# Banded attention on de-interleaved positions (even, then odd), with the band mask added by a small matmul instead of multiplied in

## The chip, the cores and the metric

One core of one Trainium2 chip. The metric is the device time of one execution in microseconds (us); lower is better. A figure "median (lowest to highest, n runs)" comes from repeated executions. Spans are from the profiled execution, which leaves out some start and end cost, so a span is about 2 us below the time.

Engines: PE is the matmul array, PEld its weight loads, DVE the vector engine, ACT the activation engine, POOL the GpSimd engine, SP the engine that here only issues DMAs. "SPq" is SP's instruction queue.

## The reference

The output is `g*a + (1-g)*b` over 2048 positions of 640 features. `a` is a gated long convolution, done with FFTs. `b` is attention of 32 heads of 20 features, in which a query looks at 8 keys, two positions apart:

```python
W, dil = 8, 2
q, k, v = qkv[0], qkv[1], qkv[2]              # each [1, 32 heads, 2048, 20]
off = jnp.arange(W) * dil
idx = pos[:, None] - off[None, :]             # keys p, p-2, ..., p-14
mask = idx >= 0
...
logits = jnp.where(mask[None, None, :, :], logits, -1e9)
attn = _softmax(logits, axis=-1)
```

The query and its keys always have the same parity. If all even positions are stored first and then all odd ones, the 8 keys are neighbours.

## The kernel before

The kernel has three stages: projections (q, k, v by matmul, and beside them a short convolution on DVE that makes `kv`), attention, and the FFT convolution. The parts that matter follow. The framework orders the instructions of every engine when the kernel is built, and it finds by itself which instruction has to wait for which: two instructions that touch the same tile are tracked by the region that each accesses.

```python
# projections; q32 and k32 are [128, 8, 2080] tiles: 4 heads x 32 rows, 8 head groups t, columns = positions
...
concurrent[1](conc_pools)        # emits the short convolution: kh loads on POOL's queue, multiply-adds on DVE
nc.gpsimd.tensor_copy(VW[:, :, :, DH], valid[:].unsqueeze(2).to_broadcast([128, NB, H]))
for t32 in (q32, k32):           # zero pads, 16 columns on either side
    nc.gpsimd.memset(t32[:, :, 0:HALO], 0.0)
    nc.gpsimd.memset(t32[:, :, HALO + S:XW], 0.0)

for which, dst in ((0, q32), (1, k32)):
    for ft in range(NDT):
        stg = pst.tile([128, S], BF, name="stg", tag="stg")          # two staging buffers
        for sc in range(4):
            ps = pp1.tile([128, 512], F32, name="pj", tag="pj", bufs=2)
            ...                                                      # five matmuls into ps
            nc.scalar.copy(stg[:, 512 * sc:512 * sc + 512], ps[:])
        for h in ...:                                                # scatter: one head's rows to its place
            nc.sync.dma_start(out=dst[32 * h4 + da:32 * h4 + da + n, t, HALO:HALO + S], in_=stg[pa:pa + n, :])
    ...
for b in range(NB):                                                  # V: 18 blocks of 128 keys
    ...                                                              # matmuls into psv, ACT copies to VW

# attention; one step = 4 blocks of 114 queries x 4 heads, 40 steps
def emit_scores(si):
    ...
    for half in range(2):                                            # two heads each
        sc = pp2.tile([128, 2, 512], F32, name=f"sc{half}", tag=f"sc{half}", bufs=1)
        for bb, b in enumerate(blocks):
            for hh in range(2):
                nc.tensor.matmul(sc[:, hh, bb * BP:bb * BP + BP], lhsT=k32[...], rhs=q32[...],
                                 start=True, stop=True, tile_position=(32 * h4, 0), skip_group_check=True)
        nc.scalar.activation(dst, src, ACT.Exp, scale=SCALE)
        nc.vector.tensor_tensor(dst, dst, band[...], ALU.mult)       # zero everything outside the band
...
    fin = pos_.tile([128, D], BF, name="fin", tag="fin")             # in out_proj
    nc.scalar.activation(fin[:], op[:, 0:D], ACT.Copy, scale=omg[:, sb:sb + 1])
```

The softmax here doesn't subtract the row's maximum and nothing guards it: scores larger than these inputs give would overflow.

## Time and profile before

402.21 us median (401.27 to 403.07, 3 runs); span of the profiled run 400.5 us. The stages, read from the timelines of ACT and DVE:

| stage | ends with | us |
|---|---|---|
| projections | last copy of q or k to `stg` starts | 105.7 |
| attention | last `fin` starts | 231.6 |
| FFT | end of the span | 400.5 |

SP's timeline shows the scatters. Columns of the timelines: start in us, length of the stretch, engine, source line, operation, destination and source, how many.

```profile
30.73 43.89 SPq L388 DMA_DIRECT2D q<-stg  x36
75.91 35.59 SPq L388 DMA_DIRECT2D k<-stg  x36
```

The table of stretches gives busy time by engine (in brackets the number of instructions), the granted PE clock, the DMA share and the bandwidth:

```profile
core 0: us, PE busy (x) PEld busy (x) DVE busy (x) ACT busy (x) POOL busy (x), PEclk, DMA share, GB/s
...
60.00:80.00 20.00, 18.04 (x106) 8.95 (x105) 14.11 (x9) 10.03 (x17) 2.21 (x5) 1.00 0.66 143
80.00:106.00 26.00, 17.65 (x62) 6.78 (x61) 25.18 (x12) 7.02 (x13) 10.16 (x13) 0.80 0.59 102
```

In attention, ACT's timeline shows one pair of exps per step; in brackets stands how long the engine had been idle and what released it:

```profile
156.18 1.75 ACT L460 ACTIVATE ET<-sc 128x912 bf16<-128x912 f32 x2 [0.28 <-PE sc L454]
158.41 1.75 ACT L460 ACTIVATE ET<-sc 128x912 bf16<-128x912 f32 x2 [0.48 <-PE sc L454]
160.81 1.75 ACT L460 ACTIVATE ET<-sc 128x912 bf16<-128x912 f32 x2 [0.64 <-PE sc L454]
```

A step takes 2.2 to 2.4 us, of which ACT waits about 0.5 us for scores. The groups of instructions that the change removes or moves (busy us, mean ns of one, idle time before them):

```profile
L461 DVE TENSOR_TENSOR ET<-ET,band 128x912 bf16<-128x912 bf16 (+1 forms) x80 | 45.4, 570 | 14.5 <-ACT ET L460 13.3
...
L426 ACT ACTIVATE fin<-op,omg 128x640 bf16<-128x640 f32 x16 | 12.7, 794 | 27.7 <-PE op L423 19.7
```

### The profile page before, as it was taken

How to read it: one execution, taken by the hardware profiler on the slowest of the kernel's cores; microseconds unless marked ns; L12 is line 12 of the kernel's file. 1: busy time of each engine (PE TensorE's matmuls, PEld its weight loads, DVE VectorE, ACT ScalarE, POOL GpSimd, SP SyncE). 2: the span in 40 equal slices, each digit the busy share in tenths (PEclk: the TensorE clock that was granted, in tenths of full speed). 3: DMA queues.
4: the chain of work that ended last, by engine and by line, in shares of the span. 5: the costliest groups of instructions: out<-in, count | busy, mean ns of one | idle time of the engine just before them, and what ended most of it. 6: DMA issues, size and time to landing. Idle time of an engine off the chain costs nothing. (4 is left out here: it accounts for less than half of the span.)

```text
span 400.5 us, 9049 instructions
## 1 busy us (share of the span) xinstructions
PE 274.8 (69%) x3958; PEld 183.9 (46%) x3958; DVE 229.0 (57%) x294; ACT 194.6 (49%) x302; POOL 91.8 (23%) x97
## 2 busy tenths in 40 slices
PE   0699999875543697978878676861766784787640
PEld 0465555332222465555545345641653573476630
DVE  0331094999698867666685307649753538083540
ACT  1025545422543758585875282860446391936310
POOL 5029502090005300000000061000046008102840
PEclk9999999989655568685859596785696697769695
DMA  8926997575334901010101079999000000000047
GB/s 235 283 75 108 163 183 172 111 156 63 68 112 90 173 19 36 18 52 2 51 2 50 34 259 275 231 291 138 0 3 2 2 2 2 2 2 4 2 95 169
DMA packets 26552, 37.37 MB, mean 93 GB/s; under 512 B 15616, under 2 KB 21364, under 8 KB 26000
## 3 DMA queue, kind: packets, MB, share of 16 engines
q1 hardware_dynamic: 21136, 19.62, 20.8%
q0 software_dynamic: 5232, 17.13, 19.7%
q8 instruction: 31, 0.51, 0.6%
q14 instruction: 9, 0.07, 0.1%
q10 hardware_dynamic: 144, 0.04, 0.0%
HBM read 26.26 MB, written 5.25 MB: 79 GB/s over the span
## 5 line engine op out<-in xcount | busy, mean ns | idle before, releaser
L460 ACT ACTIVATE ET<-sc 128x912 bf16<-128x912 f32 (+1 forms) x80 | 63.9, 855 | 21.2 <-PE O L476 11.0
L376 PE MATMUL pj<-xT,W 128*128 128x512 bf16 x200 | 49.9, 405 | 10.0 <-ACT stg L379 10.0
L308 POOL TENSOR_TENSOR a_lin<-a_lin,b_lin 128x480 bf16<-128x480 bf16 (+1 forms) x18 | 32.8, 1856 | 104.1 <-DVE a_lin L307 104.1
L461 DVE TENSOR_TENSOR ET<-ET,band 128x912 bf16<-128x912 bf16 (+1 forms) x80 | 45.4, 570 | 14.5 <-ACT ET L460 13.3
L190 PE MATMUL pb<-Am,Gre 64*128 64x80 bf16 x512 | 32.4, 233 | 27.4 <-DVE Hs L244 14.7
L196 ACT CAST Am<-pa 128x512 bf16<-128x512 f32 x80 | 41.2, 725 | 17.4 <-PE pa L190 17.4
L454 PE MATMUL sc<-q,k 20*128 20x114 bf16 x576 | 32.0, 257 | 18.8 <-ACT ET L460 17.7
L190 PEld LDWEIGHTS <-Gim 64*128 64x128 bf16 x512 | 27.9, 119 | 31.7 <-issue 31.7
L196 ACT CAST Cm<-pa 128x512 bf16<-128x512 f32 x40 | 21.0, 612 | 42.7 <-PE pa L190 42.7
L244 DVE TENSOR_TENSOR Hs<-pb,Dg 128x960 bf16<-128x960 f32 (+1 forms) x24 | 23.9, 1041 | 29.5 <-PE pb L190 29.4
L379 ACT CAST stg<-pj 128x512 bf16<-128x512 f32 x40 | 22.6, 589 | 30.8 <-PE pj L376 20.1
L376 PEld LDWEIGHTS <-W 128*128 128x128 bf16 x200 | 20.3, 103 | 35.5 <-issue 16.0
L423 PE MATMUL op<-wo,oT 128*128 128x512 bf16 (+1 forms) x160 | 33.1, 362 | 3.4 <-ACT fin L426 3.4
L190 PE MATMUL pb<-Am,Gim 64*128 64x80 bf16 x512 | 33.1, 235 | 0.0
L476 PE MATMUL O<-VW,ET 128*128 128x21 bf16 x576 | 22.4, 179 | 13.1 <-DVE o_S L485 12.8
L406 ACT CAST VW<-psv 128x640 bf16<-128x640 f32 x18 | 12.6, 700 | 36.5 <-PE psv L404 36.5
L307 DVE TENSOR_TENSOR a_lin<-pa,a_lin 128x480 bf16<-128x480 f32 (+1 forms) x24 | 13.3, 591 | 28.9 <-PE pa L190 28.9
L190 PEld LDWEIGHTS <-Gre 64*128 64x128 bf16 x512 | 28.7, 119 | 1.1 <-issue 0.8
L476 PEld LDWEIGHTS <-ET 128*128 128x128 bf16 x576 | 19.3, 102 | 18.3 <-issue 12.7
L454 PEld LDWEIGHTS <-k 20*128 20x128 bf16 x576 | 16.7, 107 | 23.2 <-issue 17.9
L190 PE MATMUL pa<-MU,Up 128*128 128x128 bf16 x160 | 24.0, 252 | 3.3 <-DVE a_lin L307 3.3
L426 ACT ACTIVATE fin<-op,omg 128x640 bf16<-128x640 f32 x16 | 12.7, 794 | 27.7 <-PE op L423 19.7
(76 smaller groups left out, 502.8 us busy)
## 6 DMA issues: line engine op xcount, KB each, us to landing
h_lin<-in_A_v_dram POOLq DMA_DIRECT2D x4, 640.0 KB, 16.2
h_lin<-in_A_ssm_k_dram POOLq DMA_DIRECT2D x8, 320.0 KB, 6.7
b_scr<-fin SPq DMA_DIRECT2D x16, 160.0 KB
W<-in_B_wqkv_dram SPq DMA_DIRECT2D x3, 800.0 KB
kh<-in_A_k_dram POOLq DMA_DIRECT2D x12, 190.0 KB, 13.1
q<-stg SPq DMA_DIRECT2D x28, 80.0 KB
k<-stg SPq DMA_DIRECT2D x28, 80.0 KB
Him<-ca_Him POOLq DMA_DIRECT2D x1, 2048.0 KB, 17.7
```

The lines of the kernel that those rows point to most:

```text
L190: inst = nc.tensor.matmul(*args, **kwargs)
L196: nc.scalar.copy(dst, src)
L244: nc.vector.tensor_tensor(Hs[:, :, :, j0:j0 + nj, :], view, Dgv.unsqueeze(3).to_broadcast([128, 2, IL, nj, 4]), ALU.add)
L307: nc.vector.tensor_tensor(reg, yv, reg, ALU.mult)
L308: (nc.vector if g == NG - 1 else nc.gpsimd).tensor_tensor(reg, reg, breg, ALU.add)
L376: nc.tensor.matmul(ps[:], lhsT=W[:, dt, which, 128 * ft:128 * ft + 128], rhs=xT[:, dt, HALO + 512 * sc:HALO + 512 * sc + 512], start=(dt = ...
L379: nc.scalar.copy(stg[:, 512 * sc:512 * sc + 512], ps[:])
L423: nc.tensor.matmul(op[:, n0:n1], lhsT=oT[:, ft, HALO + 128 * sb:HALO + 128 * sb + 128], rhs=wo[:, ft, n0:n1], start=(ft == 0), stop=(ft == ...
L454: nc.tensor.matmul(sc[:, hh, bb * BP:bb * BP + BP], lhsT=k32[32 * h4:32 * h4 + DH, t, kc:kc + 128], rhs=q32[32 * h4:32 * h4 + DH, t, qc:qc ...
L460: nc.scalar.activation(dst, src, ACT.Exp, scale=SCALE)
L461: nc.vector.tensor_tensor(dst, dst, band[:].unsqueeze(1).unsqueeze(1).to_broadcast([128, 2, nbb, BP]), ALU.mult)
L476: nc.tensor.matmul(O[:, slot * 21:slot * 21 + 21], lhsT=ET[:, h4, bb, :], rhs=VW[:, b, h, :], start=True, stop=True, skip_group_check=True)
```

## The change

The intent is to take DVE's 80 band multiplies away. With even positions stored before odd ones, 8 adjacent keys are needed instead of 8 of 15, so a block of 128 keys serves 121 queries instead of 114, and 17 blocks do instead of 18. The band is added before the exp: a matmul with 11 rows puts 0 inside the band and a large negative number outside it into the score banks, and the score matmuls accumulate on top. `fin` moves from ACT to DVE. The q and k tiles get three pads (front, between the halves, tail) of 7, 7 and 10 columns, and every scatter now writes two runs of 1024 columns. The diff, cut to its core:

```diff
-BP = 114
-NB = 18
-HALO = 16
-XW = 2080
+BP = 121
+NB = 17
+PRE = 7
+HS = 1024 + PRE
+XW = 2072
+NF = 11
+PADS = ((0, PRE), (HS, HS + PRE), (2 * HS, XW))
...
         for t32 in (q32, k32):
-            nc.gpsimd.memset(t32[:, :, 0:HALO], 0.0)
-            nc.gpsimd.memset(t32[:, :, HALO + S:XW], 0.0)
+            for c0, c1 in PADS:
+                nc.gpsimd.memset(t32[:, :, c0:c1], 0.0)
...
-                    nc.sync.dma_start(out=dst[32 * h4 + da:32 * h4 + da + n, t, HALO:HALO + S], in_=stg[pa:pa + n, :])
+                    rows = slice(32 * h4 + da, 32 * h4 + da + n)
+                    o2 = dst[rows, t, PRE:PRE + 2 * HS].rearrange("p (two c) -> p two c", two=2)[:, :, 0:S // 2]
+                    nc.sync.dma_start(out=o2, in_=stg[pa:pa + n, :].rearrange("p (two c) -> p two c", two=2))
...
-            nc.scalar.activation(fin[:], op[:, 0:D], ACT.Copy, scale=omg[:, sb:sb + 1])
+            nc.vector.tensor_scalar(fin[:], op[:, 0:D], omg[:, sb:sb + 1], None, ALU.mult)
...
-            ETb = p2.tile([128, 4, 4, 128], BF, name=f"ET{e_}")
-            nc.gpsimd.memset(ETb[:, :, :, BP:128], 0.0)
+            ETb = p2.tile([128, 2, 512], BF, name=f"ET{e_}")
+            nc.gpsimd.memset(ETb[:], 0.0)
...
-            for half in range(2):
-                sc = pp2.tile([128, 2, 512], F32, name=f"sc{half}", tag=f"sc{half}", bufs=1)
-                for bb, b in enumerate(blocks):
-                    for hh in range(2):
-                        ...                                           # scores of one half
-                nc.scalar.activation(dst, src, ACT.Exp, scale=SCALE)
-                nc.vector.tensor_tensor(dst, dst, band[:]..., ALU.mult)
+            scs = [pp2.tile([128, 2, 512], F32, name=f"sc{half}", tag=f"sc{half}", bufs=1) for half in range(2)]
+            for h4 in range(4):                                       # masks of all four heads
+                nc.tensor.matmul(scs[h4 // 2][:, h4 % 2, 0:nw], lhsT=mk[32 * h4:32 * h4 + NF, :],
+                                 rhs=mq[32 * h4:32 * h4 + NF, 0:nw], start=True, stop=False, ...)
+            for bb, b in enumerate(blocks):
+                for h4 in range(4):                                   # scores of all four heads
+                    nc.tensor.matmul(scs[h4 // 2][:, h4 % 2, bb * BP:bb * BP + BP], ..., start=False, stop=True, ...)
+            for half in range(2):
+                nc.scalar.activation(ETs[(2 * si + half) % NET][:, :, 0:nw], scs[half][:, :, 0:nw],
+                                     ACT.Exp, scale=SCALE)
```

More of the change, by code (lines that the diff above doesn't have):

```diff
@@ L68, in phase_a_consts, with ccol @@
                 Hre=_np_bf16(Hre), Him=_np_bf16(Him))
+def ccol(sb):
+    return PRE + 128 * sb + (PRE if sb >= 8 else 0)
 def phase_b_consts():
-    kl = np.arange(128)[:, None]
-    pl = np.arange(BP)[None, :]
-    dlt = kl - pl
-    band = ((dlt >= 0) & (dlt <= 14) & (dlt % 2 == 0)).astype(np.float32)
-    b = np.arange(NB)[None, :]
-    key = BP * b - 14 + np.arange(128)[:, None]
-    valid = ((key >= 0) & (key < S)).astype(np.float32)
-    ident = np.eye(128, dtype=np.float32)
-    return dict(band=_np_bf16(band), valid=_np_bf16(valid), ident=_np_bf16(ident))
+    B, C = 32768.0, 65536.0
+    kk = np.arange(128); qq = np.arange(BP)
+    kc = kk // 8 - 8; ko = kk % 8; qc = qq // 8 - 8; qo = qq % 8
+    sk = np.where(kc % 2 == 0, 1.0, -1.0); sq = np.where(qc % 2 == 0, 1.0, -1.0)
+    mk = np.zeros((4, 32, 128)); mq = np.zeros((4, 32, BP))
+    mk[:, 0] = kc * kc; mk[:, 1] = kc; mk[:, 2] = 1.0
+    mq[:, 0] = -B; mq[:, 1] = B * (2 * qc + 1); mq[:, 2] = -B * (qc * qc + qc) - C / 2
+    for v in range(8):
+        mk[:, 3 + v] = sk * (ko == v)
+        mq[:, 3 + v] = (C / 2) * sq * np.where(v < qo, -1.0, 1.0)
+    tot = np.einsum("fk,fq->kq", mk[0], mq[0])
+    dlt = kk[:, None] - qq[None, :]
+    inb = (dlt >= 0) & (dlt <= 7)
+    assert (tot[inb] == 0).all() and (tot[~inb] <= -C / 2).all()
+    for m in (mk, mq):
+        assert (_np_bf16(m).astype(np.float64) == m).all()
+    pos = BP * np.arange(NB)[None, :] - PRE + kk[:, None]
+    valid = (((pos >= 0) & (pos < 1024)) | ((pos >= HS) & (pos < HS + 1024))).astype(np.float32)
+    return dict(mk=_np_bf16(mk.reshape(128, 128)), mq=_np_bf16(np.tile(mq.reshape(128, BP), (1, 4))),
+                valid=_np_bf16(valid), ident=_np_bf16(np.eye(128)))
 def lin_src(x2, cq):
@@ L338, in b_proj @@
         W = p1.tile([128, NDT, 3, D], BF, name="W")
-        nc.gpsimd.memset(xT[:, :, 0:HALO], 0.0)
-        nc.gpsimd.memset(xT[:, :, HALO + S:XW], 0.0)
+        for c0, c1 in PADS:
+            nc.gpsimd.memset(xT[:, :, c0:c1], 0.0)
         with nc.allow_non_contiguous_dma(reason="tiny gate_w load"):
@@ L346, in b_proj @@
             xS = pxs.tile([128, 16, D], BF, name="xS")
-            xq4 = xq.rearrange("(t p) d -> p t d", p=128)
+            xq4 = xq.rearrange("(t p two) d -> p two t d", p=128, two=2)
             for c_ in range(4):
                 eng = nc.sync if c_ % 2 == 0 else nc.gpsimd
-                eng.dma_start(xS[:, 4 * c_:4 * c_ + 4, :], xq4[:, 4 * c_:4 * c_ + 4, :])
+                par, t0 = c_ // 2, 4 * (c_ % 2)
+                eng.dma_start(xS[:, 4 * c_:4 * c_ + 4, :], xq4[:, par, t0:t0 + 4, :])
             for w_ in range(3):
@@ L358, in b_proj @@
                         nc.tensor.transpose(trp[:, k_, :], xS[:, sb, 128 * dt:128 * dt + 128], ident[:, :])
-                    nc.vector.tensor_copy(xT[:, dt, HALO + 1024 * grp:HALO + 1024 * grp + 1024],
+                    nc.vector.tensor_copy(xT[:, dt, ccol(8 * grp):ccol(8 * grp) + 1024],
                                           trp[:].rearrange("p a b -> p (a b)"))
@@ L366, in b_proj @@
         for t32 in (q32, k32):
-            nc.gpsimd.memset(t32[:, :, 0:HALO], 0.0)
-            nc.gpsimd.memset(t32[:, :, HALO + S:XW], 0.0)
+            for c0, c1 in PADS:
+                nc.gpsimd.memset(t32[:, :, c0:c1], 0.0)
         for which, dst in ((0, q32), (1, k32)):
@@ L376, in b_proj @@
                         nc.tensor.matmul(ps[:], lhsT=W[:, dt, which, 128 * ft:128 * ft + 128],
-                                         rhs=xT[:, dt, HALO + 512 * sc:HALO + 512 * sc + 512],
+                                         rhs=xT[:, dt, ccol(4 * sc):ccol(4 * sc) + 512],
                                          start=(dt == 0), stop=(dt == NDT - 1))
@@ L392, in b_proj @@
                     for dt in range(NDT):
-                        nc.tensor.matmul(gps[:, sb:sb + 1], lhsT=xT[:, dt, HALO + 128 * sb:HALO + 128 * sb + 128],
+                        nc.tensor.matmul(gps[:, sb:sb + 1], lhsT=xT[:, dt, ccol(sb):ccol(sb) + 128],
                                          rhs=wg[:, dt:dt + 1], start=(dt == 0), stop=(dt == NDT - 1))
@@ L396, in b_proj @@
                 nc.vector.tensor_scalar(omg[:], g_sb[:], -1.0, 1.0, ALU.mult, ALU.add)
-                nc.gpsimd.dma_start(g_scr.rearrange("(t p) -> p t", p=128), g_sb[:])
+                for par in range(2):
+                    nc.gpsimd.dma_start(g_scr.rearrange("(t p two) -> p two t", p=128, two=2)[:, par, :],
+                                        g_sb[:, 8 * par:8 * par + 8])
         for b in range(NB):
-            c0 = HALO + BP * b - 14
+            c0 = BP * b
             psv = pp1.tile([128, 1024], F32, name="psv", tag="psv", bufs=2)
@@ L406, in b_proj, with b_attn @@
             nc.scalar.copy(VW[:, b, :, 0:DH], psv[:, 0:D].rearrange("p (h d) -> p h d", h=H))
-def b_attn(tc, B_wo, q32, k32, VW, omg, band, ident, b_scr):
+def b_attn(tc, B_wo, q32, k32, VW, omg, mk, mq, ident, b_scr):
     nc = tc.nc
+    b_rows = b_scr.rearrange("(t p two) d -> two t p d", p=128, two=2)
     with ExitStack() as es2:
@@ L422, in out_proj @@
                 for ft in range(NDT):
-                    nc.tensor.matmul(op[:, n0:n1], lhsT=oT[:, ft, HALO + 128 * sb:HALO + 128 * sb + 128],
+                    nc.tensor.matmul(op[:, n0:n1], lhsT=oT[:, ft, ccol(sb):ccol(sb) + 128],
                                      rhs=wo[:, ft, n0:n1], start=(ft == 0), stop=(ft == NDT - 1))
             fin = pos_.tile([128, D], BF, name="fin", tag="fin")
-            nc.scalar.activation(fin[:], op[:, 0:D], ACT.Copy, scale=omg[:, sb:sb + 1])
-            nc.sync.dma_start(b_scr[128 * sb:128 * sb + 128, :], fin[:])
@@ L429, in b_attn @@
-        NET = 3
+            nc.vector.tensor_scalar(fin[:], op[:, 0:D], omg[:, sb:sb + 1], None, ALU.mult)
+            nc.sync.dma_start(b_rows[sb // 8, sb % 8], fin[:])
+        NET = 6
         ETs = []
         for e_ in range(NET):
-            ETb = p2.tile([128, 4, 4, 128], BF, name=f"ET{e_}")
-            nc.gpsimd.memset(ETb[:, :, :, BP:128], 0.0)
+            ETb = p2.tile([128, 2, 512], BF, name=f"ET{e_}")
+            nc.gpsimd.memset(ETb[:], 0.0)
             ETs.append(ETb)
-        n_groups = (NB + 3) // 4
@@ L436, in b_attn @@
-        steps = [(bg, t) for bg in range(n_groups) for t in range(NT)]
+        GROUPS = [[0, 1, 2, 3], [4, 5, 6, 7], [8, 9, 10], [11, 12, 13], [14, 15, 16]]
+        steps = [(bg, t) for bg in range(len(GROUPS)) for t in range(NT)]
         o_S_tiles = {}
-        def blocks_of(bg):
-            return list(range(4 * bg, min(4 * bg + 4, NB)))
         def emit_scores(si):
             bg, t = steps[si]
-            blocks = blocks_of(bg)
-            nbb = len(blocks)
-            ET = ETs[si % NET]
-            for half in range(2):
-                sc = pp2.tile([128, 2, 512], F32, name=f"sc{half}", tag=f"sc{half}", bufs=1)
-                for bb, b in enumerate(blocks):
-                    for hh in range(2):
-                        h4 = 2 * half + hh
-                        kc = HALO + BP * b - 14
-                        qc = HALO + BP * b
-                        nc.tensor.matmul(sc[:, hh, bb * BP:bb * BP + BP],
-                                         lhsT=k32[32 * h4:32 * h4 + DH, t, kc:kc + 128],
-                                         rhs=q32[32 * h4:32 * h4 + DH, t, qc:qc + BP],
-                                         start=True, stop=True, tile_position=(32 * h4, 0), skip_group_check=True)
-                src = sc[:, :, 0:nbb * BP].rearrange("p h (b c) -> p h b c", b=nbb)
-                dst = ET[:, 2 * half:2 * half + 2, 0:nbb, 0:BP]
-                nc.scalar.activation(dst, src, ACT.Exp, scale=SCALE)
-                nc.vector.tensor_tensor(dst, dst, band[:].unsqueeze(1).unsqueeze(1).to_broadcast([128, 2, nbb, BP]), ALU.mult)
@@ new lines, in emit_scores @@
+            blocks = GROUPS[bg]
+            nw = len(blocks) * BP
+            scs = [pp2.tile([128, 2, 512], F32, name=f"sc{half}", tag=f"sc{half}", bufs=1) for half in range(2)]
+            for h4 in range(4):
+                nc.tensor.matmul(scs[h4 // 2][:, h4 % 2, 0:nw], lhsT=mk[32 * h4:32 * h4 + NF, :],
+                                 rhs=mq[32 * h4:32 * h4 + NF, 0:nw], start=True, stop=False,
+                                 tile_position=(32 * h4, 0), skip_group_check=True)
+            for bb, b in enumerate(blocks):
+                for h4 in range(4):
+                    nc.tensor.matmul(scs[h4 // 2][:, h4 % 2, bb * BP:bb * BP + BP],
+                                     lhsT=k32[32 * h4:32 * h4 + DH, t, BP * b:BP * b + 128],
+                                     rhs=q32[32 * h4:32 * h4 + DH, t, PRE + BP * b:PRE + BP * b + BP],
+                                     start=False, stop=True, tile_position=(32 * h4, 0), skip_group_check=True)
@@ L463, in emit_pv @@
+            for half in range(2):
+                nc.scalar.activation(ETs[(2 * si + half) % NET][:, :, 0:nw], scs[half][:, :, 0:nw],
+                                     ACT.Exp, scale=SCALE)
         def emit_pv(si):
             bg, t = steps[si]
-            blocks = blocks_of(bg)
+            blocks = GROUPS[bg]
             nbb = len(blocks)
-            ET = ETs[si % NET]
             if t == 0:
@@ L471, in emit_pv @@
             O = pp2.tile([128, 512], F32, name="O", tag="O", bufs=1)
-            for bb, b in enumerate(blocks):
-                for h4 in range(4):
-                    h = 4 * t + h4
+            for h4 in range(4):
+                ET = ETs[(2 * si + h4 // 2) % NET]
+                for bb, b in enumerate(blocks):
                     slot = bb * 4 + h4
-                    nc.tensor.matmul(O[:, slot * 21:slot * 21 + 21], lhsT=ET[:, h4, bb, :], rhs=VW[:, b, h, :],
-                                     start=True, stop=True, skip_group_check=True)
+                    nc.tensor.matmul(O[:, slot * 21:slot * 21 + 21], lhsT=ET[:, h4 % 2, BP * bb:BP * bb + 128],
+                                     rhs=VW[:, b, 4 * t + h4, :], start=True, stop=True, skip_group_check=True)
             nsl = nbb * 4
@@ L489, in emit_group_tail @@
         def emit_group_tail(bg):
-            blocks = blocks_of(bg)
+            blocks = GROUPS[bg]
             o_S = o_S_tiles.pop(bg)
@@ L495, in emit_group_tail @@
                     nc.tensor.transpose(tr[:, ft, 0:BP], o_S[0:BP, bb, 128 * ft:128 * ft + 128], ident[0:BP, 0:BP])
-                nc.vector.tensor_copy(oT[:, :, HALO + BP * b:HALO + BP * b + BP], tr[:, :, 0:BP])
-            pos_done = min(BP * (blocks[-1] + 1), S)
-            while 128 * (sb_done[0] + 1) <= pos_done:
+                nc.vector.tensor_copy(oT[:, :, PRE + BP * b:PRE + BP * b + BP], tr[:, :, 0:BP])
+            done = BP * (blocks[-1] + 1) + PRE
+            while sb_done[0] < 16 and ccol(sb_done[0]) + 128 <= done:
                 out_proj(sb_done[0])
@@ L509, in b_attn @@
                 emit_group_tail(bg)
-        sb_done = sb_done[0]
-        assert sb_done == 16
+        assert sb_done[0] == 16
 @with_exitstack
@@ L536 @@
     CB = phase_b_consts()
-    band_d = nc.inline_tensor(CB["band"], name="band_c")
+    mk_d = nc.inline_tensor(CB["mk"], name="mk_c")
+    mq_d = nc.inline_tensor(CB["mq"], name="mq_c")
     valid_d = nc.inline_tensor(CB["valid"], name="valid_c")
@@ L553 @@
             VW = pb0.tile([128, NB, H, 21], BF, name="VW")
-            band = pb0.tile([128, BP], BF, name="band")
+            mk = pb0.tile([128, 128], BF, name="mk")
+            mq = pb0.tile([128, 4 * BP], BF, name="mq")
             valid = pb0.tile([128, NB], BF, name="valid")
             ident = pb0.tile([128, 128], BF, name="ident")
-            nc.gpsimd.dma_start(band[:], band_d.ap())
+            nc.gpsimd.dma_start(mk[:], mk_d.ap())
+            nc.gpsimd.dma_start(mq[:], mq_d.ap())
             nc.gpsimd.dma_start(valid[:], valid_d.ap())
@@ L563 @@
                                               a_prefetch(tc, A_ssm_k, cd, h_lin, F1bd))))
-            b_attn(tc, B_wo, q32, k32, VW, omg, band, ident, b_scr)
+            b_attn(tc, B_wo, q32, k32, VW, omg, mk, mq, ident, b_scr)
         a_fft(tc, A_q, A_ssm_D, cd, kv, h_lin, F1bd, g_scr, b_scr, out)
```

## The prediction

> What bounds the kernel now. Three stages follow each other: projections (to 106 us), attention (106 to 231.5, where the last output-projection matmul ends), FFT (231.5 to 400.5). The FFT's tables load only when attention frees its memory, so what moves 231.5 moves the end. Inside attention the timeline shows no saturated engine: ACT's exp pair of a 4-block step takes 1.75 us, and one step takes 2.2 to 2.3 us with 0.5 to 0.6 us of ACT waiting for score matmuls (the score banks have one buffer per half). The band multiply (80 x 570 ns, 45 us of DVE, by the groups) is only partly on that loop. At 116 to 125.5 attention stands still: DVE finishes the convolution's kv product (ends 123.9), bands in between.
>
> What changes.
> Removed: 45 us of band on DVE, 12.7 us of `fin` on ACT (goes to DVE, where 640 elements should also take about 0.8 us). Exp area (17x121 against 18x114) and the 40 steps stay.
> Added: 160 mask matmuls, 484 or 363 columns. Two heads of a half run side by side (the trace's 114-column scores come every 25 ns warm, half their streaming time; the Trainium skill, "TensorE: Matmul & The Clock Gate", Part 3, describes such row-group concurrency). At the 0.5 clock that most attention windows show, I estimate 0.40 us per 4-block half, 0.30 per 3-block half.
> Moved, by the static order of instructions: (a) in PE order the last score of half 0 stands behind the masks and most scores of half 1, which wait for the previous exp of half 1. So per 4-block step ACT waits about 0.15+0.40+0.35+0.22 = 1.1 us cold, 0.75 warm; step 2.95 or 2.6 us against 2.25 before. 3-block steps alternate between this and a clean order: about 2.05 cold, 1.8 warm. (b) The six probability buffers are now cleared wholly (about 1.05 us each, from 657 ns for 640 columns), and POOL does it after the eight filter loads (1.19 us each), which wait for kv. The first exp waits for that. With V blocks issued before the rest of q, q scatters leave the loads' way and DVE has no bands in between, so kv should end near 111 (123.9 before); first exp near 122, fourth step near 129, against 126 before. (c) The tail has three blocks and three output projections instead of two: 4 us more, cold.
>
> Sum from the fourth step on: 5 x 2.95 + 28 + 3 x 21 = 106 us mainly cold, 93 us if wholly warm, then a tail of 13 or 11 us: attention ends at 248 or 233, against 231.5. I expect mostly cold, some warm windows around output projections: about 240.
>
> Predicted: 411 us, 80% range 400 to 422. Faster by over 2%: 0.05; within 2%: 0.45; slower by over 2%: 0.50.
>
> What would show it: the groups show no band line; ACT's exps start near 122 after waiting for POOL's clears; ACT waiting for score matmuls grows from 10 us to 25 or more; projections end no later than 106; PE busier in attention; FFT stage as long as before (169 us).
>
> What would make it wrong: the clock gate opening because masks keep the array busy (then 400 to 404); exp not really waiting for the clears, or kv ending much earlier, near 105; masks of two heads not overlapping (then 420 and more); scatters of q and k in 2 KB pieces slower than in 4 KB ones (now about 0.3 us per 4 KB packet), which would delay projections.

## More of the kernel before

The scatters of q begin at 30.73 us, while the projections still run. POOL's timeline says when the pads of q and k are cleared; in brackets stands how long the engine had been idle and what released it.

```profile
79.91 2.75 POOL L121 DMA_DIRECT2D kh<-in_A_k_dram  x4 [15.35 <-DVE tmp L133]
82.64 0.58 POOL L141 DMA_DIRECT2D F1bd<-ca_F1bd  x1
83.26 5.04 POOL L365 COPY VW<-valid 128x576 bf16<-128x576 bf16 x1
87.88 0.53 POOL L367 MEMSET q<- 128x128 bf16 x1
```

The pads of q are cleared at 87.88 us, 57 us after the first scatter into the same tile. They come so late because POOL takes its instructions in order, and the loads of `kh` in front of them wait for DVE (POOL is idle for 15.35 us before them). It costs nothing here: pads and data are different columns, and nothing waits for the clears until attention.

From 60 to 80 us PE is busy for 18.04 of 20 us, at full clock.

## The result

453.86 us median (448.89 to 454.87, 6 runs) against 401.62 us (400.55 to 403.07, 6 runs) for the kernel before; the ratio is 1.126, 95% interval 1.120 to 1.132. The result is numerically correct. Ratios in this document are the mean time of one kernel's fast runs over that of the other's of the same rounds, so not quite the ratio of the medians beside them. The prediction of 411 us, range 400 to 422, was wrong.

| stage | before | after | difference |
|---|---|---|---|
| projections, until the last `stg` copy starts | 105.7 | 149.4 | +43.7 |
| attention, from there until the last `fin` starts | 125.9 | 132.2 | +6.3 |
| rest, to the end of the span | 168.9 | 167.6 | -1.3 |
| span | 400.5 | 449.2 | +48.7 |

Nearly all of the loss is in the projections, where the change adds no work. SP's timeline of the changed kernel, then the line of SP's waits that is new (us in total, times, longest):

```profile
79.75 35.81 SPq L409 DMA_DIRECT2D q<-stg  x36
115.67 39.97 SPq L409 DMA_DIRECT2D k<-stg  x36
```

```profile
SPq L409 <- POOL k L387: 46.4, 1, 46.4
```

The first scatter goes at 79.75 us instead of 30.73. It is one wait of 46.4 us, on POOL's line 387, which is the clear of the q and k pads. The name in that line is the tile that POOL cleared last there; the count that the first scatter really waits for is read further down. POOL's timeline shows why the clear is late:

```profile
71.39 2.74 POOL L139 DMA_DIRECT2D kh<-in_A_k_dram  x4 [12.26 <-DVE tmp L151]
74.13 0.58 POOL L159 DMA_DIRECT2D F1bd<-ca_F1bd  x1
74.75 4.87 POOL L384 COPY VW<-valid 128x544 bf16<-128x544 bf16 x1
79.21 0.60 POOL L387 MEMSET q<- 128x56 bf16 x3
```

POOL's queue is as before; the clear is even 8.7 us earlier (79.21 against 87.88). What is new is that somebody waits for it. One waiting scatter holds all 36: SP issues in order. This is what the Trainium skill says in "DMA: Bandwidth & Descriptors", section "Anatomy of one DMA — SWDGE (gpsimd) path": the DMA engines do not wait on semaphores, "any semaphore wait happens on the issuing sequencer before dispatch" (the section follows a DMA that GpSimd issues; the sentence is about DMA engines in general). The trace agrees for SP's queue, with one wait of 46.4 us and no scatter in that time.

From there it spreads. There are two staging buffers; ACT fills both and then waits for scatters to empty them. ACT's timeline:

```profile
37.42 0.59 ACT L398 CAST stg<-pj 128x512 bf16<-128x512 f32 x1 [0.49 <-PE pj L395]
...
90.67 1.07 ACT L398 CAST stg<-pj 128x512 bf16<-128x512 f32 x2 [29.98 <-DMA q<-stg]
```

The V blocks, which need no scatter, fill the time to 60 us; then PE has nothing left:

```profile
core 0: us, PE busy (x) PEld busy (x) DVE busy (x) ACT busy (x) POOL busy (x), PEclk, DMA share, GB/s
...
60.00:80.00 20.00, 0.00 (x0) 0.00 (x0) 19.64 (x10) 0.70 (x1) 8.56 (x12) 0.55 0.37 75
80.00:106.00 26.00, 11.65 (x43) 4.85 (x44) 25.56 (x16) 5.66 (x10) 1.82 (x3) 0.69 0.43 68
```

PE is busy for 0.00 of the 20 us in which it did 18.04 us of work before. The projections lose 44 us.

The attention loop is slower too, as predicted. ACT's timeline of three steps, and what PE does in one of them:

```profile
171.46 1.84 ACT L479 ACTIVATE ET<-sc 128x968 bf16<-128x968 f32 x2 [1.04 <-PE sc L474]
174.35 1.84 ACT L479 ACTIVATE ET<-sc 128x968 bf16<-128x968 f32 x2 [1.05 <-PE sc L474]
177.24 1.84 ACT L479 ACTIVATE ET<-sc 128x968 bf16<-128x968 f32 x2 [1.04 <-PE sc L474]
```

```profile
172.49 0.59 PE L469 MATMUL sc<-mq,mk 11*128 11x484 bf16 x2 [0.37 <-ACT ET L479]
172.85 0.61 PE L474 MATMUL sc<-q,k 20*128 20x121 bf16 x7
173.36 0.58 PE L469 MATMUL sc<-mq,mk 11*128 11x484 bf16 x2
173.39 0.96 PE L474 MATMUL sc<-q,k 20*128 20x121 bf16 x9
174.28 0.63 PE L494 MATMUL O<-VW,ET 128*128 128x21 bf16 x16
174.35 1.84 ACT L479 ACTIVATE ET<-sc 128x968 bf16<-128x968 f32 x2 [1.05 <-PE sc L474]
```

A step is 2.89 us and ACT waits 1.05 us of it. After the masks of half 0 only seven of its eight scores are issued; the eighth stands behind the masks of half 1, which wait until ACT has read the banks of half 1 of the step before. ACT's next exp needs that eighth score. The two masks of a half run side by side, which their starts show: in this step 172.491 and 172.497 us, and wherever one mask directly follows another in the trace (85 times) 3 to 6 ns apart; the first score follows 0.35 us after the second mask. This agrees with the Trainium skill, "TensorE: Matmul & The Clock Gate", Part 3, which describes several matmuls running at once in different row groups of the array. The same page's section "Single matmul latency" has a formula for one full-array matmul at the low clock, which gives (219 + 484)/1.2 = 586 ns as an estimate; the 0.58 us that the profile shows for each mask is near it, but the ends of matmuls are modelled in this profile, so that is no test of the formula. The page of the changed kernel's profile has these groups:

```profile
L479 ACT ACTIVATE ET<-sc 128x726 bf16<-128x726 f32 (+1 forms) x80 | 64.6, 855 | 53.7 <-PE sc L474 52.1
...
L469 PE MATMUL sc<-mq,mk 11*128 11x363 bf16 (+1 forms) x160 | 34.5, 453 | 14.3 <-ACT ET L479 13.2
```

The band line is gone from DVE, and ACT's wait for scores has gone from 10.1 us in the kernel before to 52.1 us. This pair of sums overstates the loss: while `fin` is on ACT, a part of the same waiting stands in front of `fin` (27.7 us in the kernel before), and it moves to the exps when `fin` goes to DVE. Run 6 below shows how much.

### The profile page after: what moved, and what is told of

Same layout as the page of the kernel before. It is cut to its first block, busy times and chain, and to the rows that moved or that the text cites. A ratio compares the mean times of both kernels' runs of the same rounds, so it can differ in the third digit from the quotient of the medians.

```text
span 449.2 us, 9117 instructions
## 1 busy us (share of the span) xinstructions
PE 295.8 (66%) x4021; PEld 195.1 (43%) x4039; DVE 203.4 (45%) x229; ACT 184.0 (41%) x285; POOL 97.4 (22%) x105
## 5 line engine op out<-in xcount | busy, mean ns | idle before, releaser
L479 ACT ACTIVATE ET<-sc 128x726 bf16<-128x726 f32 (+1 forms) x80 | 64.6, 855 | 53.7 <-PE sc L474 52.1
L395 PE MATMUL pj<-xT,W 128*128 128x512 bf16 x195 | 52.6, 427 | 49.3 <-ACT stg L398 48.9
L499 DVE RECIPROCAL rden<-O 121x12 f32<-121x12 f32 (+1 forms) x40 | 9.6, 240 | 91.2 <-DMA k<-stg 48.7
L469 PE MATMUL sc<-mq,mk 11*128 11x363 bf16 (+1 forms) x160 | 34.5, 453 | 14.3 <-ACT ET L479 13.2
L474 PE MATMUL sc<-q,k 20*128 20x121 bf16 x544 | 40.1, 270 | 0.0
L447 PE MATMUL op<-wo,oT 128*128 128x128 bf16 (+1 forms) x151 | 29.8, 339 | 5.8 <-DVE fin L450 4.4
L474 PEld LDWEIGHTS <-k 20*128 20x128 bf16 x544 | 26.6, 117 | 9.8 <-issue 5.4
L429 ACT CAST VW<-psv 128x640 bf16<-128x640 f32 x17 | 11.8, 695 | 36.1 <-PE psv L427 36.1
L427 PE MATMUL psv<-W,xT 128*128 128x512 bf16 (+1 forms) x166 | 23.5, 297 | 3.0 <-DMA W<-in_B_wqkv_dram 2.8
```

The costliest lines, as they stand in the source:

```text
L395: nc.tensor.matmul(ps[:], lhsT=W[:, dt, which, 128 * ft:128 * ft + 128], rhs=xT[:, dt, ccol(4 * sc):ccol(4 * sc) + 512], start=(dt == 0), ...
L427: nc.tensor.matmul(psv[:, n0:n1], lhsT=xT[:, dt, c0:c0 + 128], rhs=W[:, dt, 2, n0:n1], start=(dt == 0), stop=(dt == NDT - 1))
L447: nc.tensor.matmul(op[:, n0:n1], lhsT=oT[:, ft, ccol(sb):ccol(sb) + 128], rhs=wo[:, ft, n0:n1], start=(ft == 0), stop=(ft == NDT - 1))
L469: nc.tensor.matmul(scs[h4 // 2][:, h4 % 2, 0:nw], lhsT=mk[32 * h4:32 * h4 + NF, :], rhs=mq[32 * h4:32 * h4 + NF, 0:nw], start=True, stop=F ...
L474: nc.tensor.matmul(scs[h4 // 2][:, h4 % 2, bb * BP:bb * BP + BP], lhsT=k32[32 * h4:32 * h4 + DH, t, BP * b:BP * b + 128], rhs=q32[32 * h4: ...
L479: nc.scalar.activation(ETs[(2 * si + half) % NET][:, :, 0:nw], scs[half][:, :, 0:nw], ACT.Exp, scale=SCALE)
```

## The experiments

The theory: the scatter's new destination makes it wait for the pad clears, which stand late on POOL. Of the +52 us, about 44 come from that and the rest from the attention loop. The rivals: the scatters are slower in two runs of 2 KB than in one of 4 KB; or the new order (V blocks first) or the mask matmuls cost the time. Three jobs were run, on three chips; each has its own runs of the kernel before, with medians of 401.34, 401.77 and 402.03 us.

| run | time, us | ratio to before |
|---|---|---|
| clears first | 409.93 (408.61 to 411.83) | 1.019 (1.013 to 1.025) |
| before, made to wait | 433.41 (430.58 to 435.69) | 1.077 (1.070 to 1.084) |
| clears first, half by half | 400.72 (400.11 to 403.78) | 0.997 (0.992 to 1.003) |
| the same without masks (wrong result) | 391.61 (389.17 to 392.69) | 0.972 (0.966 to 0.978) |
| half by half, band multiply | 400.95 (398.26 to 403.87) | 0.996 (0.989 to 1.004) |
| half by half, `fin` on ACT | 404.11 (403.19 to 405.27) | 1.004 (0.997 to 1.011) |
| half by half, band on half 0 and masks on half 1 | 402.42 (400.61 to 404.27) | 1.000 (0.993 to 1.006) |
| after, split scatters | 478.49 (478.07 to 483.33) | 1.192 (1.183 to 1.200) |
| after, split scatters, 8-column pads | 450.94 (449.76 to 453.63) | 1.123 (1.117 to 1.128) |
| after, middle pads cleared first | 453.35 (one look) | - |
| half by half, pads cleared by DVE | 398.64 (396.88 to 401.89) | 0.992 (0.988 to 0.997) |

### 1. Clears first

```diff
         for c0, c1 in PADS:
             nc.gpsimd.memset(xT[:, :, c0:c1], 0.0)
+        for t32 in (q32, k32):
+            for c0, c1 in PADS:
+                nc.gpsimd.memset(t32[:, :, c0:c1], 0.0)
...
         nc.gpsimd.tensor_copy(VW[:, :, :, DH], valid[:]...)
-        for t32 in (q32, k32):
-            for c0, c1 in PADS:
-                nc.gpsimd.memset(t32[:, :, c0:c1], 0.0)
```

> After, with the three zero pads of q and k cleared before the convolution's loads are issued on POOL; nothing else moves in the source. Theory (the first q scatter waits 46 us for those clears, because its two-piece destination spans the middle pad): the first scatter starts near 31 us, V blocks and q stand mixed again, projections end at 105 to 109 us instead of 150, kv ends near 118, attention takes about 120 us from its fourth step on, total 405 to 412 us. Rival 1 (2 KB scatter pieces are slow in themselves): first scatter early, but projections still end past 135 and the total stays over 435. Rival 2 (the whole loss is the attention loop): total within 10 us of after, 444 to 458.

Measured: 409.93 us, correct. SP's timeline:

```profile
33.50 46.94 SPq L409 DMA_DIRECT2D q<-stg  x36
```

The two-run scatters are as they were in the changed kernel, and so are the masks; only six small clears have moved. 44 us come back, and the last `stg` copy starts at 108.6 us. So neither the 2 KB runs nor the masks made the loss. The order of V blocks went back to the mixed one of before by itself: it was a consequence of the late scatter, not a cause. 409.93 us is also near the 411 us that the prediction gave for the whole change. Against the kernel before, run 1 is 1.3 to 2.5% slower, which is not clear of the 2% below which two kernels count as the same.

### 2. Before, made to wait

```diff
-            nc.gpsimd.memset(t32[:, :, 0:HALO], 0.0)
+            nc.gpsimd.memset(t32[:, :, 0:HALO + 1], 0.0)
```

One column more is cleared, the first of the data, so that the scatter really must come after the clear. The result stays right.

> Before, with one more column in the front pad's clear (a column that the scatter then overwrites), so that each q and k scatter must wait for POOL's clears; 4 KB pieces, band multiply, order inside attention as before. Theory: q scatters start near 76 to 80 us, projections end near 145 to 150, kv is done by then so attention loses its stall of about 10 us, total 430 to 442. Rival 1 (2 KB pieces) and rival 2 (attention loop): total stays 400 to 408.

Measured: 433.41 us, correct. SP's timeline and the new line of its waits:

```profile
76.91 35.93 SPq L388 DMA_DIRECT2D q<-stg  x36
```

```profile
SPq L388 <- POOL k L368: 46.5, 1, 46.5
```

The kernel before, with 4 KB scatters and no mask anywhere, gets the same wait (46.5 us against 46.4) from one column of one clear. The last `stg` copy starts at 144.2 us. The total loses only 32 us and not 44, because the attention that follows is 10 us shorter: the convolution's last product starts on DVE at 101.6 us and is done before attention begins, while in the kernel before it stands among the bands (`kv`, 4.45 us at 119.43). ACT's wait at the fifth step, in the kernel before and in run 2:

```profile
126.08 1.75 ACT L460 ACTIVATE ET<-sc 128x912 bf16<-128x912 f32 x2 [10.60 <-PE O L476]
155.62 1.75 ACT L460 ACTIVATE ET<-sc 128x912 bf16<-128x912 f32 x2 [1.98 <-PE O L476]
```

Runs 1 and 2 together show the cause from both sides.

### 3. Clears first, half by half

```diff
-            scs = [...]; masks of four heads; scores of four heads; two exps
+            for half in range(2):
+                sc = pp2.tile([128, 2, 512], F32, name=f"sc{half}", tag=f"sc{half}", bufs=1)
+                for h4 in (2 * half, 2 * half + 1):     # two masks
+                    ...
+                for bb, b in enumerate(blocks):         # the scores of these two heads
+                    ...
+                nc.scalar.activation(ETs[(2 * si + half) % NET][:, :, 0:nw], sc[:, :, 0:nw], ACT.Exp, scale=SCALE)
```

> e1, with masks and scores emitted half by half, so that the last score of half 0 no longer stands behind half 1's masks. Theory (that order makes ACT wait about 1.05 us per four-block step): steps fall from 2.9 to about 2.2 us (four blocks) and from 2.1 to 1.8 (three blocks), ACT's wait for score matmuls falls from 52 us to 25 or less, total 388 to 398. Rival (the masks' own time on PE is what ACT waits for): steps fall by under 0.2 us, total within 5 us of e1.

Measured: 400.72 us, correct, 9 us under run 1 and 2.7 us above the upper edge of what was expected; ACT's wait for scores is 39.1 us and not 25 or less. Undisturbed steps are short now. Two steps of run 1, then three of run 3 (the granted clock from 111 to 118 us is 0.53 in both):

```profile
114.21 1.84 ACT L479 ACTIVATE ET<-sc 128x968 bf16<-128x968 f32 x2 [1.05 <-PE sc L474]
117.10 1.84 ACT L479 ACTIVATE ET<-sc 128x968 bf16<-128x968 f32 x2 [1.05 <-PE sc L474]
...
111.20 1.84 ACT L479 ACTIVATE ET<-sc 128x968 bf16<-128x968 f32 x2
113.31 1.84 ACT L479 ACTIVATE ET<-sc 128x968 bf16<-128x968 f32 x2 [0.27 <-PE sc L475]
115.65 1.84 ACT L479 ACTIVATE ET<-sc 128x968 bf16<-128x968 f32 x2 [0.49 <-PE sc L475]
```

So the 1.05 us wait per step did come from the order in which masks and scores of the two halves were emitted. The sum of ACT's waits fell less, because part of it stands elsewhere: four waits of 3.1 to 3.9 us come while PE is busy with output projections. How the 9 us divide is not shown: later in attention the granted clock differs too (a mean of 0.72 in run 3 from 109 to 229 us, 0.65 in run 1 from 109 to 242 us).

### 4. The same without masks

The mask matmuls are left out and the scores start the banks themselves. The result is wrong (relative error 0.97).

> e4 without the mask matmuls; WRONG RESULT on purpose (no band at all). It is the price of the masks alone. If masks hide behind exp in the clean order: total within 4 us of e4. If PE is on the loop: 10 us or more faster than e4, steps of four blocks 1.9 us. I expect 380 to 388, 6 to 12 us under e4, because at the half clock a mask pair costs about 0.4 us per half and the scores wait behind it.

Measured: 391.61 us. The total missed its range by 3.6 us, but the difference of 9 us to run 3, which the range of 6 to 12 us was for, came as expected. So the masks cost 9 us even in the good order. That is just short of the 10 us set for "PE is on the loop", and far from the 4 us set for masks that hide.

### 5. Half by half, band multiply instead of masks

Run 4 with `nc.vector.tensor_tensor(..., band, ALU.mult)` after each exp, so a right result again, on the de-interleaved layout.

> e4 without mask matmuls, with a band multiply on DVE (80 of them, 484 or 363 columns by two heads) in the new layout; right result. It prices masks against band at equal layout. If masks are the cheaper way, as the change meant: slower than e4 (400.7), 403 or more. If PE is what the masks load and DVE has room: faster than e4. I expect 392 to 400: steps near 2.2 us for four blocks as in before, ACT freed of fin, but kv on DVE is again delayed by bands (about 4 us).

Measured: 400.95 us, 0.95 us above the range. With everything else equal the 160 mask matmuls and the 80 band multiplies cost about the same, some 9 us each against run 4 (run 5 is of another job; its ratio to before is that of run 3 within 0.1%, with an interval of about 0.8% to either side). The intent of the change, to trade DVE's 45 us of bands for matmuls, gains nothing that these runs can resolve: neither sum of busy time is what the loop pays.

The traces show that the bands' cost is mostly one stall. In run 5 DVE works on `kv` among the bands until 123.1 us, and ACT waits 9.11 us before the exp at 125.25 us; at the same step run 4 waits 1.14 us. From the ninth step to the last exp both take the same time (79.7 us in run 4, 79.9 us in run 5). So bands with `kv` out of their way might cost much less than 9 us; no run tried it.

### 6. Half by half, `fin` on ACT

```diff
-            nc.vector.tensor_scalar(fin[:], op[:, 0:D], omg[:, sb:sb + 1], None, ALU.mult)
+            nc.scalar.activation(fin[:], op[:, 0:D], ACT.Copy, scale=omg[:, sb:sb + 1])
```

> e4 with the scaling of the output projection back on ACT (0.79 us there, 0.88 us on DVE). If moving it to DVE was worth something: 2 to 6 us slower than e4, 403 to 407, because exp and fin queue on ACT again. If ACT's 39 us of waiting for scores absorb it: within 2 us of e4. I lean to 402 to 405.

Measured: 404.11 us, 3.4 us above run 3, which ran in another job; by the ratios to before it is 0.7%, and the two intervals overlap. So a gain of about 3 us from moving `fin`, out of 12.7 us of busy time, is likely but not shown. The page's groups tell where the waiting stands now:

```profile
L479 ACT ACTIVATE ET<-sc 128x726 bf16<-128x726 f32 (+1 forms) x80 | 64.9, 855 | 14.3 <-PE sc L475 12.4
...
L450 ACT ACTIVATE fin<-op,omg 128x640 bf16<-128x640 f32 x16 | 12.7, 794 | 31.7 <-PE op L447 28.1
```

With only `fin` moved, ACT's wait for scores is 12.4 us instead of run 3's 39.1, though the kernel is no faster. So this sum cannot be compared between kernels with `fin` on different engines, and the prediction's sign "from 10 us to 25 or more" was a weak one.

### 7. Band on half 0, masks on half 1

Half 0 has a band multiply and no masks, half 1 the other way round, to share the cost between DVE and PE.

> e4 with half 0 banded on DVE (during half 1's exp) and half 1 masked on PE: a try at a version that beats both. Theory that PE's mask time lies on the loop of each half: about half of the 9 us that masks cost (e4 against e5) comes back, 394 to 398. If the bands' place on DVE (before kv, before the reciprocals) costs as much: 399 to 402.

Measured: 402.42 us, 0.4 us above the rival's range and far from the theory's: no gain over either pure form.

### 8. After, split scatters

This asks what in the destination makes the scatter wait. Each scatter becomes two plain ones of 1024 columns; the clears stay where the change left them.

```diff
-                    nc.sync.dma_start(out=o2, in_=stg[pa:pa + n, :].rearrange("p (two c) -> p two c", two=2))
+                    for par in range(2):
+                        nc.sync.dma_start(out=o2[:, par, :], in_=stg[pa:pa + n, 1024 * par:1024 * par + 1024])
```

> After, with each q and k scatter cut in two plain scatters of one 2 KB piece per row; the clears stay late on POOL. Tells whether the wait comes from the two-piece form. Theory (a plain piece is not ordered behind the clears): no wait of the q scatter for POOL, it starts near 33 us; but 144 issues at the 0.64 to 0.77 us that one took in after need about 105 us of the SP queue, so projections end near 140 to 148 and the total is 438 to 450. Rival (any write to q and k waits for the clears, or 2 KB pieces themselves delay): first scatter near 78 us again and, with twice the issues, total over 480.

Measured: 478.49 us, missed by far, and the rival does not fit either: 14 scatters start between 33.2 and 43.5 us, and only the next one waits for POOL:

```profile
SPq L410 <- POOL k L387: 37.8, 1, 37.8
```

So the two-run form is not the whole reason. The Trainium skill advises, in "Perfetto Trace Analysis", section "Identifying Dependency Chains", to read from the instruction itself which semaphore it waits on. In the compiled program of this kernel the pieces differ: a second-half piece (columns 1038 to 2061) waits for nothing on POOL, and 14 of them are issued first; the first first-half piece (columns 7 to 1030) waits until POOL has done the clear of the middle pad of q (columns 1031 to 1037). The first scatter of the changed kernel itself waits for the same clear. No column is in both the first half and the middle pad. But in bytes, at two per element, with the boundaries that are not multiples of 4 marked by a star:

| | front pad | first half | middle pad | second half | tail pad |
|---|---|---|---|---|---|
| 7-column pads | 0 to 14* | 14* to 2062* | 2062* to 2076 | 2076 to 4124 | 4124 to 4144 |
| 8-column pads | 0 to 16 | 16 to 2064 | 2064 to 2080 | 2080 to 4128 | 4128 to 4144 |

The piece that waits shares a 4-byte word with a pad on either side; the piece that does not wait shares none. A coarser unit does not fit: 2076 and 4124 are not multiples of 8. In the kernel before, the pads of 16 columns end at multiples of 32 bytes.

### 9. After, split scatters, 8-column pads

```diff
-PRE = 7
+PRE = 8
...                                   # key windows and V blocks start one column later
-    valid = (((pos >= 0) & (pos < 1024)) | ...
+    valid = (((pos >= 0) & (pos < 1025)) | ...
```

The last line gives the one pad query that would otherwise see no key at all a denominator other than zero; it belongs to no output.

> After with pads of 8 instead of 7 columns (all boundaries of pads and data at multiples of 4 bytes; the key window starts one column later) and each scatter split into two plain pieces, clears where the change left them. Theory: a plain piece waits for a clear only if the two share a 4-byte word (with 7-column pads the piece that ends at byte 2062 shares one with the middle pad), a two-run destination is compared more coarsely; so here no scatter waits for POOL, the first goes at 31 to 34 us, 72 q pieces at 0.71 us each end near 84 us, projections end near 124 us (in the split run with 7-column pads the last copy began 39 us after the first k piece), time 424 to 438 us. Rival, that a scatter waits because POOL's clear comes earlier in the program, whatever the alignment: POOL wait of about 38 us stays and the time is 470 to 485 us as in the split run before.

Measured: 450.94 us, correct. Half of the expectation held. There is no line of POOL among SP's waits for the scatters, and the first one goes early:

```profile
31.18 63.70 SPq L410 DMA_DIRECT2D q<-stg  x72
95.00 53.71 SPq L410 DMA_DIRECT2D k<-stg  x72
```

One column more of pad takes the wait away from plain scatters, with the clears as late as ever. So where the pads' edges lie is one cause of the wait, shown by this pair of runs. That the unit is a 4-byte word rests on run 8 alone: its first 14 pieces, with edges at multiples of 4 but not of 8, went without a wait, and the next did not. The time was missed by 13 us. The 72 pieces of q took 63.7 us, not 51: their issue also waits for copies and for earlier scatters. The last `stg` copy starts at 134.3 us instead of the expected 124, and the k pieces end at 148.7, so attention has to stop and wait. ACT's timeline, and the wait of DVE that holds it:

```profile
145.60 1.84 ACT L480 ACTIVATE ET<-sc 128x968 bf16<-128x968 f32 x2 [1.05 <-PE sc L475]
159.56 1.84 ACT L480 ACTIVATE ET<-sc 128x968 bf16<-128x968 f32 x2 [12.11 <-PE O L495]
```

```profile
DVE rden L500 <- DMA k<-stg: 45.6, 1, 45.6
```

Twice as many scatters on one queue cost about as much as the wait did. That is a second price, not the same one: against run 1 the last `stg` copy starts 25.7 us later, and attention takes 11 us more. The second part is this stop. DVE had nothing to do before, so only the end of its wait counts. It ends at 158.26 us, 9.6 us after the last k piece was issued; POOL's filter loads, issued from 139.6 us, are in flight with the last pieces, and the DMA engines are busy without a gap from 148 to 160 us (share 1.04).

### 10. After, middle pads cleared first

```diff
+        for t32 in (q32, k32):        # early
+            nc.gpsimd.memset(t32[:, :, PADS[1][0]:PADS[1][1]], 0.0)
...
-            for c0, c1 in PADS:
+            for c0, c1 in (PADS[0], PADS[2]):
```

> After with only the middle pads of q and k cleared early, front and tail pads where the change left them; two-run scatters as in the change. Theory (a two-run destination is compared coarsely, so front and tail clears hold it as well as the middle one): the first q scatter still goes only near 76 to 80 us after a wait for POOL of about 46 us, time 445 to 456 us. Rival, that the middle pad alone is at fault because it lies between the two runs: first scatter near 33 us, time 405 to 412 us.

Measured: 453.35 us in one look (a single run, so its state is unknown), first scatter at 79.85 us after a wait for POOL of 46.3 us, as the theory had it. The middle pad alone is not at fault. In the compiled program the first scatter of this kernel waits for the front pad's clear, and the first one of head group 1 for the tail's.

What stays open is the exact rule for the two-run destination. A kernel with two-run scatters and 8-column pads was built, not run: its scatters still wait for POOL, for the middle pad's clear and then for the tail's, although no word is shared. So the two-run form seems to be compared more coarsely than a plain one. But this is read from one program, and no run separates the possible rules. It is not needed for the cause of the loss: runs 1 and 2 show that. The waits told here and under run 8 stand in no trace.

### 11. Half by half, pads cleared by DVE

In run 3 POOL issues the load of x 1 us later than before (5.14 against 4.09 us), behind the six clears and the load of a second mask table. Here DVE, idle until 14 us, clears the pads of q and k, and both mask tables load after the projections.

> The half-by-half kernel with the pad clears of q and k on DVE (idle until 14 us) and the two mask tables loaded after the projections, so that POOL issues the x load at once (4.1 us instead of 5.1). First transposes 1 us earlier, first q scatter near 31 to 32 us instead of 33.5, projections end near 106.5; 397 to 400 us, that is 0.5 to 1.5 % under the kernel before. Rival (the start is bound by the load's bandwidth, not by its issue, or the loads of the tables collide with the filter loads): no gain, 400 to 402 us.

Measured: 398.64 us, ratio 0.992 (0.988 to 0.997), correct: as expected. The first q scatter goes at 31.13 us, the last `stg` copy starts at 104.9 us. This is the lowest median with a right result, 0.8% under the kernel before, within the 2% that counts as the same. Its interval overlaps that of run 3, so the step from run 3 to run 11 is not shown to be a gain. It has all of the change's parts, with its two faults mended.

## Why the prediction was wrong

Point by point, from the prediction's own list:

- **"Projections end no later than 106": failed, and this is the step that made the prediction wrong.** They ended at 149.4 us (last `stg` copy). The prediction costed the scatters by their size only ("scatters of q and k in 2 KB pieces slower than in 4 KB ones") and took the waits in front of them as unchanged. In their place the runs showed a new wait of 46.4 us for clears that had always been late but that nobody had waited for. Mending it alone gives 409.93 us.
- The sign was in hand: the prediction used the static order "V blocks issued before the rest of q" as a gain. That order was new, and it was there because q's scatter had to wait. It should have led to the question what the scatter waits for.
- "First exp near 122", behind POOL's clears of the probability buffers: failed. In the changed kernel projections end later than the filter loads. In run 1, where they end at 108.6, the first exp starts at 111.31; there the static order has the clears in front of the filter loads, so the feared chain was not tried as predicted. In the changed kernel `kv` was done near 109 us (POOL's loads of `h_lin`, which wait for it, start at 109.37), close to the predicted 111.
- Step (a), the order of masks and scores: right in mechanism and size. Predicted 2.95 us per 4-block step at the low clock with 1.1 us of ACT waiting; measured 2.89 and 1.05. Run 3 shows that the order is the reason.
- The mask's cost: predicted 0.40 us per half; from the start of the masks to the first score in the trace is 0.36 us (172.49 to 172.85). `fin` on DVE takes 0.88 us; predicted was 0.8. The granted clock did not rise with the masks: its mean in attention is 0.66 in the kernel before (106 to 232 us) and 0.67 in the changed one (150 to 282 us).
- Attention as a whole: predicted to end at 240 after projections at 106, thus 134 us; measured 132.2 us. Part of this is luck, because two misses cancel. The fourth step was predicted 23 us after the projections (129 after 106) and came 11.8 us after them (161.19 after 149.4). From there to the end 111 us were predicted and 120.4 measured (161.19 to 281.6).
- FFT as before: right, 167.6 us against 168.9.

So the prediction of 411 us comes out for a kernel that differs from the changed one only in where six clears stand, though by the same two misses: in run 1 the fourth step starts at 120.0 us instead of 129, and attention needs 122 us from there instead of 111. Of the loss of 52 us, 44 are the wait with what follows from it (difference of run 1 to the changed kernel). The remaining 8 us (run 1 to before) lie in attention, which takes 133.8 us in run 1 and 125.9 before; run 3, in which nothing but the order of masks and scores differs from run 1, takes 9 us back.

Where the intended gain went: the removed bands were worth about 9 us of their 45 us of busy time (run 5 against run 4), and the masks cost 9 us (run 3 against run 4). `fin` on DVE gains perhaps 3 us (run 6, not clear of the noise). The change could therefore win at most a few us, and run 11 shows what is left: 3 us.

## What to carry to other kernels

A clear, a load or a copy that stands late on an in-order engine is harmless only as long as nobody waits for it. When a change touches the shape of an access or the edges of a region, even by one column, look again at what each DMA waits for, not only at its bytes. Put the clears of pads at the very start, on an engine that is idle there. And when the static order of another engine changes without being asked to (here the V blocks), find the reason before counting it as a gain.

## What the Trainium skill lacked or had wrong

- "DMA: Bandwidth & Descriptors" says that a DMA's waits happen on the issuing sequencer, and the trace agrees; it lacks what follows for a row of DMAs: one wait of 46.4 us held 36 scatters and cost 44 us in the end (run 1), and 72 scatters of half the size in place of 36 kept one queue busy for 63.7 us instead of 46.9 and put the last copy at 134.3 us instead of 108.6 (run 9 against run 1).
- No page says that writes to different columns of one tile can be made to wait for each other. Here a plain DMA waited for a clear whose edge lay in the same 4-byte word (7-column pads, 37.8 us), and did not with 8-column pads. "SBUF — State Buffer", section "Operand start alignment", says that DMAs into SBUF write exactly the intended bytes at addresses that are 2 bytes past a 4-byte boundary, but of GpSimd, which does the clear, it names reads of SBUF alone; so whether the wait protects anything stays open, and no run here tried to do without it.
- "TensorE: Matmul & The Clock Gate", Part 1, section "What's actually happening", has the full clock after one busy window of about 3.4 us. In the changed kernel's attention the profile shows PE busy for 12.86 of 15 us from 165 to 180 us, and for 9.25 of 10 us from 200 to 210 us, both at a granted clock of 0.50. The busy share of such small matmuls in the profile, whose ends are modelled, did not tell what clock was granted; no run here tells why, and this does not show the page wrong.
